# Attention followed by a gated MLP on one core: in the last batch, 32 by 32 block transposes on VectorE and a trip through DRAM in place of TensorE transposes

## Chip, cores and metric

The kernel runs on one core of a Trainium2 chip. The time is the device time of one execution in microseconds (us); a kernel's time is the median of its runs. The profile comes from one more execution, whose own time is named below.

## What is computed

```python
scores = scale * np.matmul(q, k.transpose(0, 1, 3, 2))      # (4, 12, 448, 64) each, fp32
scores = np.where(mask, -1000000000.0, scores)              # causal
attn = np.exp(scores - max) ; attn = attn / attn.sum
attn_out = np.matmul(attn, v)
x = attn_out.transpose(0, 2, 1, 3).reshape(1792, 768)
g = x @ w_gate ; val = x @ w_val                            # 768 -> 1536
out = (g * sigmoid(g) * val) @ w_out                        # 1536 -> 768
```

## The kernel before

The four batches are four chunks of 448 tokens. For each chunk, `attention(u)` runs once per head (a unit `u`; heads go in pairs, the even one with `h % 2 == 0`), and `moe(c)` is the MLP of the chunk. The attention of the last batch, b = 3, is spread between the MLP matmuls of the batch in front of it (b = 2).

Every piece of work is an `op` with the engines that it may run on, a cost, a due time and the buffers that it takes. A `Planner` goes through them and gives each engine its order; the instructions are then written in that order, and at run time each engine takes its own queue strictly in order. SP's queue issues the DMAs.

One head goes through these steps. `score` (L512): three fp32r matmuls per row block of a pair into PSUM tiles `S`. `rowmax` (L563, VectorE) adds the mask and takes the maximum of the row into `p`; `expo` (L575, ScalarE); `recip` (L587, L588, VectorE); `na`, `npl` or `nd` (L620, L624, L628) scales the rows of `p`. Then p, whose partitions are queries, must have keys on its partitions: `transp` (L710) makes three 128x128 TensorE transposes for key block 1 and three for blocks 2 and 3, and `transp0` (L678) four for the 64 keys of block 0, both heads of the pair at once, all into PSUM tiles `T`. `spread` copies each `T` to `ph` rounded to fp32r (L317 on ScalarE, L320 on VectorE) and puts the rest, `T` minus `ph`, into `pl` (L339). `weigh` multiplies by v: seven matmuls (L752) into the PSUM tile `O`, then a copy `tmp` and a sum into `xs`, from which `xh` and `xl` are split for the MLP.

The MLP's matmuls come in threes (L885 to L887), 448 columns each, 18 of them for one PSUM tile `M`. Their weights `whl` come by DMA from DRAM (L837, 768 KB each, five buffers); a load waits until TensorE is done with the buffer's last user.

Of the kernel before, what the change touches and what calls it, by code (L numbers as in the profile page):

```python
# [8 lines left out]
F32 = mybir.dt.float32  # L9
F32R = mybir.dt.float32r  # L10
U32 = mybir.dt.uint32
U16 = mybir.dt.uint16
# [4 lines left out]

P = 128
D = 64
BIG = -8.0e9  # L20
CUTS = [[0, 64, 192, 320, 448], [0, 64, 192, 320, 448], [0, 64, 192, 320, 448], [0, 64, 192, 320, 448]]
WID = [0, 64, 192, 320, 448]
# [25 lines left out]
TV = 0.0  # L48
WINDOW = 96
SPARE = [2]  # L50
FEW = 72
WARM = 22
WARM2 = 8
FIRST = [[[0, 1]], [[2]], [[3]]]
KBUS = 1 / 320
DLAT = 1.8
CAPS = {'S': 2, 'X': 2, 'T': 1, 'O': 1, 'M': 2, 'qraw': 3, 'kraw': 3, 'vraw': 3, 'QS': 1, 'KS': 1, 'VS': 3, 'ph': 2, 'pl': 2, 'p': 2, 'tmp': 2, 't': 3, 'osb': 2, 'wide': 3, 'wraw': 2, 'whl': 5}


def nat(flags, b, h):  # L60
# [17 lines left out]


class Op:  # L80
    __slots__ = ("port", "kind", "soft", "kb", "alts", "due", "deps", "alloc", "uses", "extra", "idx", "nd", "outs", "start", "end", "eng", "fn")

    def __init__(self, alts, due, deps, alloc, uses, extra):
        self.alts, self.due, self.alloc, self.uses, self.extra = alts, due, alloc, uses + alloc, extra
        self.deps = [d for d in deps if d is not None]
        self.port = False
        self.outs = []
        self.nd = len(self.deps)
        for d in self.deps:
            d.outs.append(self)  # L90
        for r in self.uses:
            r.left += 1


class Planner:
# [9 lines left out]
    def run(self, caps):  # L105
        free = dict.fromkeys(("PE", "DVE", "ACT", "POOL", "SP"), 0.0)
        ring = {}
        lock = {"DVE": 0.0, "POOL": 0.0}
        wire = 0.0
        kind = None  # L110

        def begin(o, e, t):
            if e == "POOL":
                return max(t, lock["DVE"])
            if e == "DVE" and o.port:
                return max(t, lock["POOL"])
            return t

        def slots(tag):
            if tag not in ring:  # L120
                c = caps.get(tag.rstrip("0123456789"), 1)
                ring[tag] = [None] * c
            return ring[tag]

        avail = {e: [] for e in free}

        def push(o):
            for e in o.alts:
                avail[e].append(o)
            dirty.update(o.alts)  # L130

        def ready(o, e):
            t = 0.0
            for d in o.deps:
                x = d.end if d in o.soft else d.end + d.extra + (LAT[d.eng] if d.eng != e else (0.0 if e == "PE" else 0.13))
                if x > t:
                    t = x
            for i, r in enumerate(o.alloc):
                h = slots(r.tag)[sum(x.tag == r.tag for x in o.alloc[:i])]
                if h is not None:  # L140
                    if h.left:
                        return None
                    if h.end > t:
                        t = h.end
            return t

        def extra(o, f):
            return BIAS.get(f, 0.0) + (SHARED if f == "DVE" and o.port else 0.0)

        def finish(o, e, s):  # L150
            best = s + o.alts[e][0] + extra(o, e)
            for f in o.alts:
                if f != e:
                    r = ready(o, f)
                    if r is not None and begin(o, f, max(r, free[f])) + o.alts[f][0] + extra(o, f) + 1e-6 < best:
                        return False
            return True

        def choose(e):
            lst = avail[e]  # L160
            lst.sort(key=lambda o: (o.due, o.idx))
            cand = []
            for o in lst[:WINDOW]:
                r = ready(o, e)
                if r is not None:
                    s = begin(o, e, max(r, free[e]))
                    if len(o.alts) == 1 or finish(o, e, s):
                        cand.append((s, o))
            if not cand:
                return None  # L170
            lim = max(min(s for s, _ in cand), free[e]) + DELTA[e]
            if e == "PE" and kind == "t":
                for s, o in cand:
                    if s <= lim and o.kind == "t":
                        return s, o
            for s, o in cand:
                if s <= lim:
                    return s, o
            return None

        dirty = set(free)
        for o in self.ops:
            if o.nd == 0:
                push(o)
        order = []
        left = len(self.ops)
        while left:
            best = None
            for e in free:
                c = choose(e)  # L190
                if c is not None and (best is None or (c[0], c[1].due) < (best[0], best[1].due)):
                    best = (c[0], c[1], e)
            assert best is not None
            s, o, e = best
            for f in o.alts:
                avail[f].remove(o)
            o.start, o.eng = s, e
            o.end = s + o.alts[e][0] * (GF if e == "POOL" else PF if e == "DVE" and o.port else 1.0)
            if e == "PE":
                o.end += TURN.get((kind or o.kind) + o.kind, 0.0)  # L200
                kind = o.kind
            o.fn = o.alts[e][1]
            free[e] = o.end
            if e == "SP":
                wire = max(wire, o.end) + o.kb * KBUS
                o.extra = wire + DLAT - o.end
            if e == "POOL" or (e == "DVE" and o.port):
                lock[e] = o.end
            for r in o.alloc:
                q = slots(r.tag)  # L210
                q.pop(0)
                q.append(r)
            for r in o.uses:
                r.left -= 1
                r.end = max(r.end, o.end + o.extra + LAT[e])
            for d in o.outs:
                d.nd -= 1
                if d.nd == 0:
                    push(d)
            order.append(o)  # L220
            left -= 1
        return order


def raw(t):
    return t.bitcast(F32)
# [3 lines left out]
def kernel(  # L230
# [115 lines left out]
    class Unit:  # L346
        def __init__(self, c, b, h, qa, qb, col):
            self.c, self.b, self.h, self.qa, self.qb, self.col = c, b, h, qa, qb, col
            cuts = CUTS[b]
            blocks = list(zip(cuts[:-1], cuts[1:]))  # L350
            self.kb = [e for e in blocks if e[0] < qb]
            self.qi = [(i, e) for i, e in enumerate(blocks) if qa <= e[0] < qb]
            self.rows = [e[1] - e[0] for _, e in self.qi]
            self.n = qb - qa
            self.ns, self.np = nat(NS, b, h), nat(NP, b, h)
            self.joint = self.ns and self.np
            self.own = [(i, e) for i, e in self.qi if i or h % 2 == 0 or not self.joint]

        def slot(self, j):
# [38 lines left out]
    def attention(u):  # L398
# [4 lines left out]
        nj = len(U.kb)  # L403
        frac = U.w0 / done_w[c]
        base = LEN[0] * FRAC0 * frac if c == 0 else start[c] + FRAC * LEN[c] * frac
        due = dues[u] = lambda stage: base + (SLOPE if c else SLOPE0) * stage
        if h % 2 == 0:
            def make(nm):
# [49 lines left out]
        if not npv:  # L458
            rV = Res("VS")

            def newv():
# [2 lines left out]
            v1 = op(copies("sbuf", nj * D, newv, lambda: s["v"]), due(8), [lv], [rV], [rv])  # L464
            v2 = op(binary(nj * D, lambda: s["VS"][:, :, D : 2 * D], lambda: s["v"],
                           lambda: raw(s["VS"])[:, :, 0:D]), due(9), [v1], [], [rV, rv])

        def peak(i):
            if "m" not in s:
# [58 lines left out]
        for i, (q0, q1_) in U.own:  # L528
# [17 lines left out]
            rp = ptile[u, i] if h % 2 else Res(f"p{sl}")  # L546
            so, rS = scored[u, i]
            new = h % 2 == 0
            if new and r < P:

                def newp(i=i, q1_=q1_, sl=sl):
                    s[f"pp{i}"] = st[u + 1][f"pp{i}"] = buf([P, 2 * q1_], F32, f"p{sl}", "p", f"p{u}_{i}")
# [81 lines left out]
        prps[u] = rps  # L634
        blocks = parts[u] = {}
        normed[u] = norms

        def spread(g, js, tr, rT, lo_row, kn, n, cols, offs, v2):

# [86 lines left out]
        if h % 2:  # L726
            weigh(u)

    def weigh(u):
        U = units[u]  # L730
        c, b, h, N = U.c, U.b, U.h, U.n
# [2 lines left out]
        k = h // 2  # L734
        prevx = [xlast[k]] if k in xlast else []
        if not npv:
            rO, dps, use, dur = Res("O"), [], [], 0.0
            for g, o_, w, _, stk, d_, r_ in (blocks[j] for j in range(nj)):
                dps += [x for x in d_ if x not in dps]
                use += [r for r in r_ if r not in use]  # L740
# [2 lines left out]
            todo = [(j, "ph") for j in (0, *range(2, nj))] + [(j, "pl") for j in range(nj - 1, 0, -1)] + [(1, "ph")]  # L743

            def pv():
                s["O"] = bank("O", f"O{u}")


                for x, (j, t) in enumerate(todo):
                    g, o_, w, _, stk, _, _ = blocks[j]  # L750
                    m = FEW if t == "pl" else 2 * D
                    nc.tensor.matmul(s["O"][:m, U.base(j) - U.qa : N], s["VS"][:, j, :m], s[f"{t}{g}"][:, o_ : o_ + w],  # L752
                                     start=x == 0, stop=x == len(todo) - 1)
            last = op({"PE": (dur, pv), "kind": "o"}, due(10), dps, [rO], use)
            rx, rt = Res(f"xs{h}"), Res("tmp")

# [280 lines left out]
```

## Time and profile before

| | |
|---|---|
| median of 3 runs | 674.75 us (674.54 to 675.5) |
| the profiled execution, its own time | 674.35 us |
| its span from first to last instruction | 672.5 us |
| TensorE busy | 666.1 us, 99% of the span |
| VectorE, ScalarE, GpSimd busy | 373.0, 357.4, 210.5 us |
| moved by DMA | 165.08 MB, 245 GB/s in the mean |

Matmuls are pipelined, so that the busy time of single ones overlaps; what a stretch of TensorE work costs is read from the distance between starts. The span is 1.85 us shorter than the execution's time.

### The profile page before, as it was taken

How to read it: one execution, taken by the hardware profiler on the slowest of the kernel's cores; microseconds unless marked ns; L12 is line 12 of the kernel's file. 1: busy time of each engine (PE TensorE's matmuls, PEld its weight loads, DVE VectorE, ACT ScalarE, POOL GpSimd, SP SyncE). 2: the span in 40 equal slices, each digit the busy share in tenths (PEclk: the TensorE clock that was granted, in tenths of full speed). 3: DMA queues.
4: the chain of work that ended last, by engine and by line, in shares of the span. 5: the costliest groups of instructions: out<-in, count | busy, mean ns of one | idle time of the engine just before them, and what ended most of it. 6: DMA issues, size and time to landing. Idle time of an engine off the chain costs nothing.

```text
span 672.5 us, 11031 instructions
## 1 busy us (share of the span) xinstructions
PE 666.1 (99%) x3906; PEld 601.9 (89%) x3906; DVE 373.0 (55%) x924; ACT 357.4 (53%) x877; POOL 210.5 (31%) x255
## 2 busy tenths in 40 slices
PE   9999999999999999999999999999999999999997
PEld 6568999999999999999999999999999999999997
DVE  5778978988886666766664355645534222222100
ACT  7998888789675674665653435545435211111000
POOL 3763445445333342462433314323422000000000
PEclk9999999999999999999999999999999999999999
DMA  8868886978958898968789766564466666656771
GB/s 292 302 197 283 305 272 241 310 263 309 353 186 304 287 318 275 313 213 300 266 298 342 268 205 211 160 208 158 148 211 207 214 207 228 210 215 232 221 244 42
DMA packets 45302, 165.08 MB, mean 245 GB/s; under 512 B 5056, under 2 KB 14528, under 8 KB 45248
## 3 DMA queue, kind: packets, MB, share of 16 engines
q1 hardware_dynamic: 45088, 164.29, 72.1%
q8 instruction: 31, 0.51, 0.3%
q14 instruction: 23, 0.19, 0.1%
q10 hardware_dynamic: 160, 0.10, 0.1%
HBM read 116.39 MB, written 47.97 MB: 244 GB/s over the span
## 4 chain that ended last, share of the span: by engine, by line
PE 95%; ACT 3%; DMA 0%; DVE 0%; issue 0%; POOL 0%; ACTq 0%; DVEq 0%
PE M L885 17%; PE M L886 17%; PE M L887 17%; PE MO L885 9%; PE MO L886 9%; PE MO L887 9%; PE S L512 6%; PE O L752 5%; PE T L710 4%; PE O L783 1%; PE T L678 1%; ACT p L575 1%; ACT p L620 1%; DMA kraw<-in_k_dram 0%; POOL p L624 0%
## 5 line engine op out<-in xcount | busy, mean ns | idle before, releaser
L885 PE MATMUL M<-xh,whl 128*128 128x448 f32 x576 | 215.3, 374 | 0.0
L886 PE MATMUL M<-xl,whl 128*128 128x448 f32 x576 | 209.3, 363 | 0.0
L887 PE MATMUL M<-xh,whl 128*128 128x448 f32 x576 | 209.1, 363 | 0.0
L887 PEld LDWEIGHTS M<-xh,whl 128*128 128x128 f32 x576 | 108.1, 188 | 7.7
L885 PEld LDWEIGHTS M<-xh,whl 128*128 128x128 f32 x576 | 108.2, 188 | 7.2 <-issue 0.3
L886 PEld LDWEIGHTS M<-xl,whl 128*128 128x128 f32 x576 | 108.4, 188 | 6.4
L885 PE MATMUL MO<-hh,whl 128*128 128x448 f32 x288 | 107.2, 372 | 0.0
L886 PE MATMUL MO<-hl,whl 128*128 128x448 f32 x288 | 104.6, 363 | 0.0
L887 PE MATMUL MO<-hh,whl 128*128 128x448 f32 x288 | 104.5, 363 | 0.0
L575 ACT ACTIVATE p<-p,m 128x192 f32<-128x192 f32 (+3 forms) x180 | 91.3, 512 | 3.0 <-DVE m L563 2.9
L563 DVE CUSTOM_DVE_ANT_0 p<-S,masks 128x192 f32<-128x192 f32 (+3 forms) x180 | 68.0, 426 | 16.2 <-PE S L512 15.8
L317 ACT ACTIVATE ph<-T 128x384 fp32r<-128x384 f32 (+3 forms) x93 | 46.6, 510 | 56.3 <-PE T L678 34.3
L317 ACT ACTIVATE hh<-t 128x448 fp32r<-128x448 f32 x43 | 24.8, 577 | 71.2 <-DVE t L928 71.2
L620 ACT ACTIVATE p<-p,rec 128x320 f32<-128x320 f32 (+3 forms) x136 | 59.9, 501 | 4.5 <-DVE rec L588 4.5
L339 DVE TENSOR_TENSOR whl<-wraw,whl 128x768 fp32r<-128x768 f32 x58 | 57.6, 993 | 7.1 <-ACT whl L317 5.9
L928 DVE TENSOR_TENSOR t<-t,M 128x448 f32<-128x448 f32 x48 | 29.7, 619 | 50.3 <-PE M L887 49.6
L922 DVE SCALAR_TENSOR_TENSOR t<-t,M 128x448 f32<-128x448 f32 x48 | 29.7, 619 | 50.2 <-ACT t L918 49.9
L887 PEld LDWEIGHTS MO<-hh,whl 128*128 128x128 f32 x288 | 54.0, 188 | 3.8
L885 PEld LDWEIGHTS MO<-hh,whl 128*128 128x128 f32 x288 | 54.1, 188 | 3.4
L886 PEld LDWEIGHTS MO<-hl,whl 128*128 128x128 f32 x288 | 54.2, 188 | 3.2
L918 ACT ACTIVATE t<-M 128x448 f32<-128x448 f32 x48 | 26.0, 542 | 47.0 <-PE M L887 46.2
L339 DVE TENSOR_TENSOR pl<-T,ph 128x384 fp32r<-128x384 f32 x72 | 39.6, 550 | 18.0 <-ACT ph L317 17.3
(81 smaller groups left out, 869.3 us busy)
## 6 DMA issues: line engine op xcount, KB each, us to landing
whl<-ws SPq DMA_DIRECT2D x72, 768.0 KB, 4.4
wide<-in_w_dram SPq DMA_DIRECT2D x36, 768.0 KB, 6.6
ws<-whl SPq DMA_DIRECT2D x36, 768.0 KB, 4.3
wr<-wraw SPq DMA_DIRECT2D x36, 384.0 KB, 3.5
wraw<-wr SPq DMA_DIRECT2D x36, 384.0 KB, 4.9
vraw<-in_v_dram SPq DMA_DIRECT2D x24, 256.0 KB, 3.6
out_dram<-osb SPq DMA_DIRECT2D x24, 224.0 KB, 4.5
qraw<-in_q_dram SPq DMA_DIRECT2D x23, 224.0 KB, 3.8
```

Source lines behind the costliest of these rows:

```text
L317: nc.scalar.activation(out(), in_(), AF.Copy, scale=scale)
L339: r["DVE"] = (cost("DVE", "two", n), lambda: nc.vector.tensor_tensor(out(), a(), b(), alu))
L512: nc.tensor.matmul(st[u + y][f"S{i}"][:r], Q[:, q0 : q0 + r], K[:, :q1_] if y else K[:, S - q1_ :], start=z == 0, stop=z == len(passes) - 1)
L563: nc.vector.tensor_tensor_reduce(p[:r], s[f"S{i}"][:r], mask[:r, maskX - q0 : maskX - q0 + q1_] if h % 2 else back[:r, P - min(q1_, P) : P ...
L575: nc.scalar.activation(p[:r], p[:r], AF.Exp, bias=peak(i)[:r], scale=-1.0, accum_out=sums[u % NR][:r, i : i + 1],)
L620: nc.scalar.activation(p[:r], p[:r], AF.Copy, scale=rec[u % NR][:r, i : i + 1])
L752: nc.tensor.matmul(s["O"][:m, U.base(j) - U.qa : N], s["VS"][:, j, :m], s[f"{t}{g}"][:, o_ : o_ + w], start=x == 0, stop=x == len(todo) - 1)
L885: nc.tensor.matmul(out[:, :n], a[:, w], xhi, start=first, stop=False)
L886: nc.tensor.matmul(out[:, :n], a[:, w], xlo, start=False, stop=False)
L887: nc.tensor.matmul(out[:, :n], l[:, w], xhi, start=False, stop=last)
L922: nc.vector.scalar_tensor_tensor(t, t, 1.0, ps[c, f, 0][:, :N], ALU.add, ALU.mult)
L928: nc.vector.tensor_tensor(t, t, ps[c, f, 1][:, :N], ALU.mult)
```

## The change

For the batches in `VIA`, here the last alone, `turn` replaces the TensorE transposes and `spread`. `blockwise` has VectorE transpose each 32x32 block of p in its place, 128 columns (four blocks) an instruction, from `p` into a buffer `w`: six instructions for the even head, ten for the odd one. `out` writes `w` to DRAM by 4 DMAs (even) or 10 (odd) so that the blocks come to lie under each other, `back` reads it all into SBUF by one DMA, and `pair` makes `ph` and `pl` from it. The queries of a row block come out in another order, which stays until the output; the host puts the columns of that batch back in order. The odd head's read also holds block 0 of both heads. `weigh` reads `ph` and `pl` by four pieces for key blocks 2 and 3. The due times of that batch's attention are 8 us earlier, and the odd head's `O` takes the PSUM bank that held `T`.

```diff
+VIA = [3]
+VLEAD = 8.0
+HOP = 0.8
...
                 wire = max(wire, o.end) + o.kb * KBUS
-                o.extra = wire + DLAT - o.end
+                o.extra = wire + DLAT + (HOP if o.hop else 0.0) - o.end
...
+        if U.via:
+            base -= VLEAD
...
+        if U.via:
+            turn(u, s, U, due, norms, rps)
...
+        n3 = 3 * G
...
+        nS = 3 * n3 + G if odd else 2 * n3
+        tps = []
+        for i in range(0 if odd else 1, 4):
+            def blockwise(i=i):
...
+                r = U.rows[i]
+                for t in range(i, 2 * i + 1) if odd else range(i):
...
+                    nc.vector.transpose(s["stage"][:r, :, at : at + G],
+                                        s[f"pp{i}"][:r, P * t : P * t + P].rearrange("p (c n) -> p c n", c=4))
...
+        row = 4 * n3 + 2 * G if odd else 0
+        ND = row + 8 * n3 if odd else 8 * n3
+
+        def out():
+            d = s["d"] = dpool.tile([P, ND], F32, tag=rD.tag, name=f"{rD.tag}{u}", bufs=CAPS[rD.tag])
+            to = d.rearrange("(c i) n -> i c n", c=4)
+            for b in range(4):
+                f = s["stage"][G * b : G * b + G]
+                if odd:
+                    nc.sync.dma_start(to[:, :, n3 * b : n3 * b + n3], f[:, :, :n3])
+                    if b < 2:
+                        nc.sync.dma_start(to[:, :, 4 * n3 + G * b : 4 * n3 + G * b + G], f[:, :, 3 * n3 :])
+                nc.sync.dma_start(to[:, :, row + 2 * n3 * b : row + 2 * n3 * (b + 1)], f[:, :, n3 * odd : n3 * odd + 2 * n3])
...
+            t = s["w"][:, 0 if odd else 4 * nS :][:, :ND]
+            s["turned"] = t
+            nc.sync.dma_start(t, s["d"])
...
+            hi = op(copies("sbuf", n, newh, view), due(8), [tr], [rh], [res])
...
+            lo = op(binary(n, newl, view, lambda: part(raw(s[f"ph{g}"])[r0 : r0 + kn])), due(9), [hi],
...
-            rO, dps, use, dur = Res("O"), [], [], 0.0
+            rO, dps, use, dur = Res("T" if U.via and h % 2 else "O"), [], [], 0.0
...
+                    if U.via:
+                        o, p = s["O"][:m, :N], s[f"{t}{g}"]
+                        if j:
+                            o, p = (x_[:, : 12 * G].rearrange("p (b n) -> p b n", b=4) for x_ in (o, p))
+                            o = o[:, :, G * (j - 1) :]
+                            p = p[:, :, : 3 * G - G * (j - 1)] if j < 3 else p[:, :, 2 * G :]
```

In the orders below a row is an instruction, its output, its inputs and its size; a name ends in a number that the program gave. On TensorE before, this is the end of an even head of the last batch, its product with v (`O`), and one group of the odd head's transposes behind it, between MLP matmuls (`M`).

```order
L887 MATMUL M_16_5466<-xh_82,whl_5270 128x448
L752 MATMUL O_5503<-ph_0_5486,VS_5078 128x448
L752 MATMUL O_5503<-ph_2_5425,VS_5078 128x256
L752 MATMUL O_5503<-ph_2_5425,VS_5078 128x128
L752 MATMUL O_5503<-pl_2_5430,VS_5078 72x128
L752 MATMUL O_5503<-pl_2_5430,VS_5078 72x256
L752 MATMUL O_5503<-pl_1_5406,VS_5078 72x384
L752 MATMUL O_5503<-ph_1_5399,VS_5078 128x384
L710 MATMUL T_1_5515<-ident,p_1_5324 128x128
L710 MATMUL T_1_5515<-ident,p_2_5326 128x128
L710 MATMUL T_1_5515<-ident,p_3_5333 128x128
L885 MATMUL M_17_5524<-xh_77,whl_5370 128x448
```

In the change the same head's product stands there with the odd head's product right behind it (L868 is the matmul of `weigh`, L1000 to L1002 the MLP's).

```order
L1002 MATMUL M_17_5612<-xh_80,whl_5400 128x448
L868 MATMUL O_5649<-ph_0_5591,VS_5140 128x448
L868 MATMUL O_5649<-ph_2_5507,VS_5140 128x4x64
L868 MATMUL O_5649<-ph_2_5507,VS_5140 128x4x32
L868 MATMUL O_5649<-pl_2_5542,VS_5140 72x4x32
L868 MATMUL O_5649<-pl_2_5542,VS_5140 72x4x64
L868 MATMUL O_5649<-pl_1_5512,VS_5140 72x384
L868 MATMUL O_5649<-ph_1_5505,VS_5140 128x384
L868 MATMUL O_5659<-ph_0_5581,VS_5442 128x448
```

The 96 transposes of the last batch are gone from TensorE; 4 of the 7 products of a head now take four pieces, with as many columns as before.

On SP's queue before, at the start of the last batch's attention, there are only weight loads, an output store and the inputs of the next pair.

```order
L960 DMA out_dram<-osb_5_4711 128x448
L837 DMA whl_4778<-ws_160 128x1536
L422 DMA qraw_4795<-in_q_dram 128x448
L422 DMA kraw_4809<-in_k_dram 128x448
L837 DMA whl_4824<-ws_161 128x1536
L837 DMA whl_4872<-ws_162 128x1536
L837 DMA whl_4895<-ws_163 128x1536
```

In the change, at the same place, the first pair's writes (`dE` even, `dO` odd) and reads stand between them (L952 is the weight load, L796 the read).

```order
L786 DMA dE_4799<-w_4783 32x4x192 x4
L952 DMA whl_4824<-ws_160 128x1536
L783 DMA dO_4843<-w_4814 32x4x96
L785 DMA dO_4843<-w_4814 32x4x32
L786 DMA dO_4843<-w_4814 32x4x192
...
L783 DMA dO_4843<-w_4814 32x4x96
L786 DMA dO_4843<-w_4814 32x4x192
L796 DMA w_4783<-dE_4799 128x768
L952 DMA whl_4880<-ws_161 128x1536
L952 DMA whl_4888<-ws_162 128x1536
L952 DMA whl_4911<-ws_163 128x1536
L796 DMA x_4941<-dO_4843 128x1216
```

Three weight loads now stand behind the odd head's ten writes and the even head's read, and the odd head's read stands behind those three.

## Rows read from the trace of the kernel before

**Rows 1.** The page: span, busy time by engine, TensorE in 40 slices.

```profile
span 672.5 us, 11031 instructions
...
PE 666.1 (99%) x3906; PEld 601.9 (89%) x3906; DVE 373.0 (55%) x924; ACT 357.4 (53%) x877; POOL 210.5 (31%) x255
...
PE   9999999999999999999999999999999999999997
```

**Rows 2.** Three stretches: length, busy time by engine, granted clock, DMA share, GB/s.

```profile
345.60:369.00 23.40, 23.40 (x142) 21.77 (x143) 12.67 (x36) 12.16 (x33) 9.84 (x11) 1.00 0.91 318
...
430.00:456.00 26.00, 26.00 (x159) 24.01 (x158) 13.10 (x37) 13.01 (x34) 7.97 (x12) 1.00 0.54 182
...
540.00:672.50 132.50, 128.86 (x645) 120.63 (x643) 22.40 (x36) 16.78 (x30) 0.00 (x0) 1.00 0.62 203
```

**Rows 3.** TensorE's timeline around one transpose group: start, duration, instruction.

```profile
437.70 0.36 PE L886 MATMUL M<-xl,whl 128*128 128x448 f32 x1
437.90 0.36 PE L887 MATMUL M<-xh,whl 128*128 128x448 f32 x1
438.10 0.49 PE L710 MATMUL T<-ident,p 128*128 128x128 f32 x3
438.35 0.45 PE L885 MATMUL M<-xh,whl 128*128 128x448 f32 x1
438.63 0.37 PE L886 MATMUL M<-xl,whl 128*128 128x448 f32 x1
```

**Rows 4.** The critical chain, 425 to 457 us: start, time on the chain.

```profile
430.03 1.72 PE S L512 x22
...
438.26 0.33 PE T L710 x3
...
448.54 0.44 PE T L678 x4
448.98 0.21 PE M L885
...
451.45 0.93 PE O L752 x7
```

**Rows 5.** VectorE's groups by form, 369 to 540 us.

```profile
L563 DVE CUSTOM_DVE_ANT_0 p<-S,masks 128x192 f32<-128x192 f32 x12 | 4.1, 345 | 0.0
...
L563 DVE CUSTOM_DVE_ANT_0 p<-S,masks 64x64 f32<-64x64 f32 x12 | 2.6, 214 | 12.5 <-PE S L512 12.5
```

**Rows 6.** Timelines of VectorE and ScalarE behind the scores of one pair.

```profile
405.16 0.22 DVE L563 CUSTOM_DVE_ANT_0 p<-S,masks 64x64 f32<-64x64 f32 x1 [1.18 <-PE S L512]
...
409.33 1.01 ACT L620 ACTIVATE p<-p,rec 128x192 f32<-128x192 f32 x2
...
412.93 1.36 ACT L620 ACTIVATE p<-p,rec 64x64 f32<-64x64 f32 x3 [0.95 <-DVE rec L588]
...
422.99 1.09 ACT L317 ACTIVATE ph<-T 64x448 fp32r<-64x448 f32 x2 [1.60 <-PE T L678]
```

**Rows 7.** The page on DMA: packets, the main queue, issues with time to landing.

```profile
DMA packets 45302, 165.08 MB, mean 245 GB/s; under 512 B 5056, under 2 KB 14528, under 8 KB 45248
...
q1 hardware_dynamic: 45088, 164.29, 72.1%
...
whl<-ws SPq DMA_DIRECT2D x72, 768.0 KB, 4.4
...
wr<-wraw SPq DMA_DIRECT2D x36, 384.0 KB, 3.5
wraw<-wr SPq DMA_DIRECT2D x36, 384.0 KB, 4.9
```

**Rows 8.** SP's queue: one issue, and its waits from 365 to 545 us.

```profile
427.70 0.33 SPq L422 DMA_DIRECT2D vraw<-in_v_dram  x1
...
SPq L837 <- PE M L887: 87.2, 24, 7.6
```

**Rows 9.** Tile T: TensorE transposes into contiguous (L710) and split (L676) columns.

```profile
L710 PE MATMUL T<-ident,p x288: 270/272/331, 10.3 to 534.5; 128*128 128x128 f32 x144
...
L676 PE MATMUL T<-ident,p x6: 271/300/329, 11.4 to 49.0; 128*128 128x128 f32 x6
```

More of the change, by code (lines that the diff above doesn't have):

```diff
@@ L19 @@
 D = 64
+G = 32
 BIG = -8.0e9
@@ L56 @@
 DLAT = 1.8
-CAPS = {'S': 2, 'X': 2, 'T': 1, 'O': 1, 'M': 2, 'qraw': 3, 'kraw': 3, 'vraw': 3, 'QS': 1, 'KS': 1, 'VS': 3, 'ph': 2, 'pl': 2, 'p': 2, 'tmp': 2, 't': 3, 'osb': 2, 'wide': 3, 'wraw': 2, 'whl': 5}
+CAPS = {'S': 2, 'X': 2, 'T': 1, 'O': 1, 'M': 2, 'qraw': 3, 'kraw': 3, 'vraw': 3, 'QS': 1, 'KS': 1, 'VS': 3, 'ph': 2, 'pl': 2, 'p': 2, 'tmp': 2, 't': 3, 'osb': 2, 'wide': 3, 'wraw': 2, 'whl': 5, 'dE': 2, 'dO': 2}
 def nat(flags, b, h):
@@ L80 @@
 class Op:
-    __slots__ = ("port", "kind", "soft", "kb", "alts", "due", "deps", "alloc", "uses", "extra", "idx", "nd", "outs", "start", "end", "eng", "fn")
+    __slots__ = ("hop", "port", "kind", "soft", "kb", "alts", "due", "deps", "alloc", "uses", "extra", "idx", "nd", "outs", "start", "end", "eng", "fn")
     def __init__(self, alts, due, deps, alloc, uses, extra):
@@ L85, in __init__ @@
         self.deps = [d for d in deps if d is not None]
-        self.port = False
+        self.port = self.hop = False
         self.outs = []
@@ L356, in __init__ @@
             self.joint = self.ns and self.np
+            self.via = b in VIA
             self.own = [(i, e) for i, e in self.qi if i or h % 2 == 0 or not self.joint]
@@ L466, in attention @@
                            lambda: raw(s["VS"])[:, :, 0:D]), due(9), [v1], [], [rV, rv])
+            s["v2"] = (v2, rV)
         def peak(i):
@@ L548, in attention @@
             new = h % 2 == 0
-            if new and r < P:
+            if new and r < P and not U.via:
                 def newp(i=i, q1_=q1_, sl=sl):
@@ L636, in attention @@
         normed[u] = norms
+        if U.via:
+            turn(u, s, U, due, norms, rps)
+            if h % 2:
+                st[u - 1]["later"]()
+                weigh(u - 1)
+                weigh(u)
+            return
         def spread(g, js, tr, rT, lo_row, kn, n, cols, offs, v2):
@@ L727, in attention, with turn, back, pair @@
             weigh(u)
+    def turn(u, s, U, due, norms, rps):
+        h, blocks = U.h, parts[u]
+        odd = h % 2
+        n3 = 3 * G
+        rS = Res("wide")
+        wide = lambda nm: buf([P, 4 * WC + 4], U16, "wide", "wide", nm).bitcast(F32)
+        nS = 3 * n3 + G if odd else 2 * n3
+        tps = []
+        for i in range(0 if odd else 1, 4):
+            def blockwise(i=i):
+                if "stage" not in s:
+                    s["w"] = wide(f"w{u}")
+                    s["stage"] = s["w"][:, : 4 * nS].rearrange("p (c n) -> p c n", c=4)
+                r = U.rows[i]
+                for t in range(i, 2 * i + 1) if odd else range(i):
+                    j = t - i if odd else i - t
+                    at = n3 * odd + n3 * (j >= 2) + G * (2 if j == 3 else i - j) if j else (3 * n3 if i == 0 else G * (i - 1))
+                    nc.vector.transpose(s["stage"][:r, :, at : at + G],
+                                        s[f"pp{i}"][:r, P * t : P * t + P].rearrange("p (c n) -> p c n", c=4))
+            k = i + 1 if odd else i
+            deps = [norms[i]] + ([normed[u - 1][i]] if odd else [])
+            new = not tps
+            o = op({"DVE": (k * (0.06 + P / 960), blockwise)}, due(6.2), deps + tps[:1], [rS] * new, [rps[i]] + [rS] * (not new))
+            o.soft = o.soft + tps[:1]
+            tps.append(o)
+        rD = Res("dO" if odd else "dE")
+        row = 4 * n3 + 2 * G if odd else 0
[10 more added lines that the diff above has]
+                nc.sync.dma_start(to[:, :, row + 2 * n3 * b : row + 2 * n3 * (b + 1)], f[:, :, n3 * odd : n3 * odd + 2 * n3])
+        wr = op({"SP": (3.4 if odd else 1.4, out), "kb": 800 if odd else 450}, due(6.4), tps, [rD], [rS])
+        wr.hop = True
+        rP = Res("wide") if odd else rS
+        def back():
+            if odd:
+                s["w"] = wide(f"x{u}")
+            t = s["w"][:, 0 if odd else 4 * nS :][:, :ND]
+            s["turned"] = t
+            nc.sync.dma_start(t, s["d"])
+        rd = op({"SP": (0.35, back), "kb": ND // 2}, due(6.6), [wr], [rP] if odd else [], [rD] + ([] if odd else [rS]))
+        rd.hop = True
+        v2, rV = s["v2"]
+        N = U.n
+        def pair(g, view, res, r0, kn, n, tr):
+            stk = kn == D
+            rh = Res(f"ph{g}")
+            part = (lambda t: t) if stk else (lambda t: t.rearrange("p (b n) -> p b n", b=4))
+            def newh():
+                s[f"ph{g}"] = buf([P, n], F32R, f"ph{g}", "ph", f"ph{u}_{g}")
+                return part(s[f"ph{g}"][r0 : r0 + kn])
+            hi = op(copies("sbuf", n, newh, view), due(8), [tr], [rh], [res])
+            rl = None if stk else Res(f"pl{g}")
+            def newl():
+                if stk:
+                    return s[f"ph{g}"][D - r0 : P - r0]
+                s[f"pl{g}"] = buf([P, n], F32R, f"pl{g}", "pl", f"pl{u}_{g}")
+                return part(s[f"pl{g}"])
+            lo = op(binary(n, newl, view, lambda: part(raw(s[f"ph{g}"])[r0 : r0 + kn])), due(9), [hi],
+                    [] if stk else [rl], [res, rh])
+            for j in ([0], [1], [2, 3])[g]:
+                blocks[j] = (g, 0, N if stk else 4 * G * (4 - j), slice(0, P), stk, [hi, lo, v2], [rh, rV] + ([] if stk else [rl]))
+        groups = lambda k: lambda: s["turned"][:, row : row + 8 * n3].rearrange("p (b n) -> p b n", b=4)[:, :, n3 * k : n3 * k + n3]
+        if odd:
+            joint = lambda r0: lambda: s["turned"][r0 : r0 + D, :N]
+            pair(0, joint(D), rP, D, D, N, rd)
+            def later():
+                e = st[u - 1]
+                e["first"](joint(0), rP, rd)
+            st[u - 1]["later"] = later
+        else:
+            s["first"] = lambda view, res, tr: pair(0, view, res, 0, D, N, tr)
+        for g in (1, 2):
+            pair(g, groups(g - 1), rP, 0, P, 4 * n3, rd)
@@ L745, in pv @@
             def pv():
-                s["O"] = bank("O", f"O{u}")
+                s["O"] = bank(rO.tag, f"O{u}")
                 for x, (j, t) in enumerate(todo):
@@ L751, in pv @@
                     m = FEW if t == "pl" else 2 * D
-                    nc.tensor.matmul(s["O"][:m, U.base(j) - U.qa : N], s["VS"][:, j, :m], s[f"{t}{g}"][:, o_ : o_ + w],
-                                     start=x == 0, stop=x == len(todo) - 1)
+                    o, p = s["O"][:m, U.base(j) - U.qa : N], s[f"{t}{g}"][:, o_ : o_ + w]
+                    if U.via:
[4 more added lines that the diff above has]
+                            p = p[:, :, : 3 * G - G * (j - 1)] if j < 3 else p[:, :, 2 * G :]
+                    nc.tensor.matmul(o, s["VS"][:, j, :m], p, start=x == 0, stop=x == len(todo) - 1)
             last = op({"PE": (dur, pv), "kind": "o"}, due(10), dps, [rO], use)
@@ L1035 @@
     r = _run(nc, [arrays], core_ids=[0])
-    return _np.ascontiguousarray(r.results[0]["out_0_dram"].T)
+    out = r.results[0]["out_0_dram"].T.copy()
+    for b in VIA:
+        x = _np.arange(S)
+        q = _np.where(x < S - D, CUTS[b][1] + x % 96 // G * P + x // 96 * G + x % G, x - (S - D))
+        out[b * S + q] = out[b * S + x]
+    return _np.ascontiguousarray(out)
```

## The prediction

> **What bounds the kernel.** The page first: TensorE is busy for 99% of the span, all but the first and last slices at nine tenths, while VectorE and ScalarE have nearly half of theirs free [rows 1]. Busy time of pipelined matmuls can hide gaps, so I read stretches next. In 430 to 456 us, one pair of the last batch, TensorE has no idle time at the full clock, VectorE and ScalarE are busy for 13 of 26 us, DMA for 0.54 [rows 2]. So in the stretch that the change touches TensorE's own queue is the limit and every microsecond taken from it shortens the run, if nothing that it then waits for is late.
>
> **What is removed.** Two MLP matmuls in a row start 0.20 us apart. Across a group of three transposes the starts are 438.10 (the group), 438.35 and 438.63 [rows 3]: from the group's start to the second matmul it is 0.53 us where 0.20 is normal, so the group costs 0.33 us, and the critical chain gives the same 0.33; the group of four costs 0.44 [rows 4]. A pair has four groups of three and one of four: 4 x 0.33 + 0.44 = 1.76 us. Six pairs: **10.56 us**. Behind the group of four the chain also shows twelve MLP matmuls in 451.45 - 448.98 = 2.47 us instead of 2.40 [rows 4]; if that goes as well it is 0.07 x 6 = 0.4 us more. I take nothing for it.
>
> **What TensorE gets instead.** The product with v keeps its columns, but 4 of its 7 matmuls read and write four pieces. The nearest row is the transpose into split columns, 300 ns against 272 [rows 9]: at most 0.028 x 4 x 12 heads = 1.3 us. I take 0, since the split row comes from six instructions in another part of the kernel whose extremes (271 to 329) are those of the unsplit row; 1.3 is the other end.
>
> **VectorE.** 16 block transposes a pair, 128 columns each. No row shows one. The mask-and-maximum instruction takes 214 ns for 64 columns and 345 for 192 [rows 5]; halfway is 280 ns, and with such instructions starting some 0.07 us before the last one ends I count 0.25 us apart: 1.5 us for the even head, 2.5 for the odd one, 4 us a pair on an engine with 13 us free [rows 2]. The copies out of PSUM that go make up for part. Nothing of it lies on TensorE's path by itself; it counts in the chain below.
>
> **DMA and SP.** Per pair 14 writes and 2 reads: 16 issues of 0.33 us [rows 8], 5.3 us of SP's queue in 26. Even: 512 runs of 768 bytes (393 KB); odd: 512 runs of 384, 256 of 128 and 512 of 768 bytes (1280 runs, 623 KB). Written and read that is 2.03 MB in 26 us, 78 GB/s on top of 182; the sum of 260 is below the 318 that an earlier stretch moved with no gap on TensorE [rows 2]. Bandwidth is not the question; the time of short runs is. Nothing before has such DMAs. From below by bytes: 318 GB/s at a share of 0.91 is 350 in all, 21.8 a DMA engine, so an odd run of 486 bytes in the mean takes 22 ns. From above: a packet of this kernel takes 0.721 x 16 x 672.5 / 45088 = 0.172 us [rows 1, 7], and it carries 3.6 KB. I take **0.05 us a run**, nearer to the bytes because the packets here are seven times as long: 80 odd runs on each of 16 engines are then 4.0 us, between 1.8 and 13.8.
>
> **Does the product with v find its operands?** This decides. All that follows counts from the end of a pair's scores, by the pair whose scores end just ahead of 405.16 [rows 6]. Even rows are scaled by 410.34, +5.2; odd ones by 414.29, +9.2. Even: transposes to +6.7, four issues to +8.0. Odd: transposes to +11.7, ten issues to +15.0. In the first pair SP has the even read behind these: issued at +15.3, landed 4.9 us later (the 384 KB reload [rows 7]) at +20.2. The odd writes land at +18.5 (3.5 us after the last issue, the 384 KB store [rows 7]; 4 us of runs from +11.7 on, with the same latency, end about there too). The odd read goes out at +18.8 and lands at +23.7; if the weight loads ahead of it have bunched up, two more of 2.25 us each (768 KB at 350 GB/s) make it +28.2. Then two copies to `ph` (1.09 us [rows 6]), one subtraction and the handing over between engines, about 2 us: the even head's operands stand at **+25.7 to +30.2**.
>
> TensorE comes to that product, by the order of the change, after 147, 168, 138, 150, 141 and 147 MLP matmuls in the six pairs, beside other scores (1.72 us) and products (0.93 [rows 4]): 31.1, 37.2, 31.2, 33.6, 31.8 and 31.2 us. The cover is 0.9 to 5.4 us longer than the chain in the tightest pairs. The odd head's product comes at once or three matmuls later and needs two more copies and subtractions, split over engines, so its slack is about half a microsecond less. I therefore expect little waiting: 1 us in all.
>
> **What is queued behind the new waits.** SP holds weight loads while it waits for the transposes. Before, SP waits for TensorE to free a buffer (24 waits, 87.2 us in the stretch [rows 8]), so loads go out as early as they can. Five buffers of 18 matmuls at 0.20 us are 18 us; less the buffer in use (3.6) and the load itself (4.4 [rows 7]) a load can be 10 us late. SP is held from about +8 to +15.3, some 7 us: covered at no cost, and each microsecond above 10 would be one on TensorE. On ScalarE the copies that wait for a read stand ahead of exponentials of the next pair and of the MLP's tanh, which frees an `M` bank; they come late only when the product does, and the two waits then overlap.
>
> **Sum.** Profiled execution 674.35 - 10.56 + 1.0 = 664.8 us. Its span of 672.5 becomes 662.9 with the same 1.85 us around it. The median of the runs is 0.4 us above the profiled execution: **665.2 us**. No waiting and the 0.4 of rows 4 give 663.8; the split columns at their upper end and 0.5 us of waiting a pair give 668.5.
>
> **A rule against the change.** The critical chain prices a transpose on TensorE at 0.11 us (0.33 for three) on the engine that is full [rows 1, 4]. The Trainium skill, "VectorE: DVE Perf Modes", section "Rules for kernel authors", says to do a 128x128 transpose on TensorE if PSUM will do as its destination, and to use VectorE for 32x32 blocks. By the row the removed work is worth 10.56 us; by the rule the trip that joins the blocks should cost more than that and the time would end above 674.75. The rule counts the transpose itself, not which engine is full, so I go by the row.
>
> **Rivals.**
> (a) *Late trip, part given back.* What speaks for it: all six pairs depend on the trip, the tightest slack is under 1 us, and ten issues in a row may wait for earlier ones' semaphores. At 0.09 us a run the odd write ends 80 x 0.04 = 3.2 us later; less a slack of about 2 us it is 1.2 us a pair, 7 on top of 664.2 without waiting: 671.4.
> (b) *Short runs cost like packets, slower than before.* The place is the odd write, the wait is in front of the even head's product. The gain is 1.76 us a pair; with 2 us of slack it is gone when the write is 3.8 us late, at 0.05 + 3.8/80 = 0.097 us a run. At 0.13 it is 6.4 - 2 - 1.76 = 2.6 us a pair worse, 16 in all: 690; at the upper bound of 0.172 it is 9.8 - 3.76 = 6 us a pair: 711. Against it: the run lengths are a seventh of the packets'.
> (c) *Short runs are done twice.* The trace's packets under 512 bytes are too few and too mixed to price [rows 7]. If a run under 512 bytes needs two passes, 48 of the 80 odd runs on an engine cost another 0.05 us: 2.4 us later, 0.4 us a pair beyond the slack of 2, 2.4 in all, or 9 with the slack at 0.9: 667 to 674. The Trainium skill, "DMA: Bandwidth & Descriptors", section "Specifications", says that below 512 B an SDMA engine reads, modifies and writes.
> (d) *SP holds the weights too long.* If SP is held 12 us instead of 7, each pair loses 2 us: 676. Against it: 10 us of cover per load.
>
> **Chances.** Forecast as summed, 663 to 668.5: 0.60, with the mild end of (c) in it. Part given back, 668.5 to 673.4 ((a), the far end of (c)): 0.18. Within 0.2% of before, 673.4 to 676.1 ((a) at its break-even): 0.08. Slower ((b), (d)): 0.14. About 0.2% is what a measurement of this kernel can tell from no change. Faster is then 0.78, same 0.08, slower 0.14. The range from 663.0 to 674.0 leaves out 0.18: (b), (d) and most of the even case.
>
> **What would show it.** Right: no TensorE transposes in the last 300 us; MLP matmuls 0.20 us apart through the last batch; no idle time on TensorE in front of its products; the MLP of the last chunk starting about 10 us sooner and taking as long; odd reads landing at most 28 us behind their scores. Wrong: idle time of TensorE released by the subtractions into `ph` or by a DMA into `x`, equal in each pair (a, b, c), or by `whl` (d); odd writes that land over 8 us after their first issue; products of a head above 0.93 us (split columns); block transposes far from 0.25 us.

## The result

The changed kernel takes **664.73 us** (median of 4 runs, 663.92 to 666.8); the kernel before, run beside it, 675.05 us. The ratio is 0.9852, with an interval of 0.9827 to 0.9877: 10 us faster. 665.2 us was forecast.

The page of the changed kernel, its first lines and its main DMA queue (share of 16 engines), answers to [rows 1] and [rows 7]:

```profile
span 662.5 us, 11097 instructions
...
PE 655.9 (99%) x3810; PEld 592.9 (90%) x3810; DVE 383.1 (58%) x999; ACT 359.3 (54%) x885; POOL 214.5 (32%) x262
...
PE   9999999999999999999999999999999999999997
...
q1 hardware_dynamic: 58912, 176.48, 78.1%
```

96 matmuls are gone from TensorE, which is as full as before; VectorE has 10 us more work, which costs nothing. The span is 10.0 us shorter. The timelines place it: the last chunk's MLP starts at 529.0 us instead of 539.1, and takes 133.4 us in both.

Three stretches of the changed kernel (columns as in [rows 2]), the middle one with the third pair of the last batch:

```profile
400.00:430.00 30.00, 30.00 (x171) 27.95 (x170) 18.94 (x67) 17.34 (x46) 12.10 (x19) 1.00 0.88 296
430.00:456.00 26.00, 25.87 (x153) 23.84 (x152) 16.57 (x51) 14.45 (x39) 10.73 (x15) 1.00 0.82 268
...
530.00:662.50 132.50, 128.78 (x644) 120.50 (x643) 22.93 (x37) 16.78 (x30) 0.00 (x0) 0.99 0.61 203
```

TensorE has no idle time but 0.13 us in the middle stretch; DMA is at 0.82 to 0.88 in the first two instead of 0.60 and 0.54. The critical chain shows that one place. It leaves TensorE and goes through the trip of the third pair (start, time on the chain; L783 and L796 are the odd head's writes and the reads, L327 and L346 GpSimd's copy and subtraction):

```profile
431.38 5.69 DMA dO<-w
437.09 0.30 SPq L783
...
439.52 8.24 DMA x<-dO
447.91 0.57 POOL ph L327
448.56 0.57 POOL ph L327
449.20 1.16 POOL ph L346
450.43 1.17 POOL ph L346
451.64 2.12 PE O L868 x14
```

The last matmul ahead of this product starts at 451.15, so that 451.35 would have been its time: it waited 0.29 us for GpSimd, which takes 1.16 us for a subtraction where VectorE takes 0.65 (the mean of nine of the same form). In the other five pairs nothing waits.

### The profile page after: what moved, and what is told of

Same layout as the page of the kernel before. It is cut to its first block, busy times and chain, and to the rows that moved or that the text cites. A ratio compares the mean times of both kernels' runs of the same rounds, so it can differ in the third digit from the quotient of the medians.

```text
span 662.5 us, 11097 instructions
## 1 busy us (share of the span) xinstructions
PE 655.9 (99%) x3810; PEld 592.9 (90%) x3810; DVE 383.1 (58%) x999; ACT 359.3 (54%) x885; POOL 214.5 (32%) x262
## 4 chain that ended last, share of the span: by engine, by line
PE 91%; ACT 3%; DMA 3%; POOL 1%; DVE 1%; issue 1%; SPq 0%; ACTq 0%; DVEq 0%; POOLq 0%
PE M L1000 16%; PE M L1001 16%; PE M L1002 16%; PE MO L1000 9%; PE MO L1001 9%; PE MO L1002 9%; PE S L520 6%; PE O L868 5%; PE T L726 3%; PE O L898 1%; ACT p L583 1%; DMA x<-dO 1%; ACT p L628 1%; PE T L694 1%; DMA dO<-w 1%
## 5 line engine op out<-in xcount | busy, mean ns | idle before, releaser
L1000 PE MATMUL M<-xh,whl 128*128 128x448 f32 x576 | 213.9, 371 | 0.0
L1002 PE MATMUL M<-xh,whl 128*128 128x448 f32 x576 | 209.0, 363 | 0.0
L1002 PEld LDWEIGHTS M<-xh,whl 128*128 128x128 f32 x576 | 108.1, 188 | 7.6
L1000 PEld LDWEIGHTS M<-xh,whl 128*128 128x128 f32 x576 | 108.2, 188 | 7.5 <-issue 0.3
L1000 PE MATMUL MO<-hh,whl 128*128 128x448 f32 x288 | 106.6, 370 | 0.0
L1002 PE MATMUL MO<-hh,whl 128*128 128x448 f32 x288 | 104.5, 363 | 0.0
L571 DVE CUSTOM_DVE_ANT_0 p<-S,masks 128x192 f32<-128x192 f32 (+3 forms) x180 | 67.6, 425 | 15.4 <-PE S L520 15.1
L1037 DVE SCALAR_TENSOR_TENSOR t<-t,M 128x448 f32<-128x448 f32 x48 | 29.7, 618 | 48.8 <-ACT t L1033 48.4
L1002 PEld LDWEIGHTS MO<-hh,whl 128*128 128x128 f32 x288 | 54.0, 188 | 3.8
L1000 PEld LDWEIGHTS MO<-hh,whl 128*128 128x128 f32 x288 | 54.1, 188 | 3.4
L321 ACT ACTIVATE ph<-T 128x384 fp32r<-128x384 f32 (+3 forms) x74 | 36.8, 510 | 27.9 <-PE T L694 17.3
L632 POOL TENSOR_SCALAR p<-p,rec 128x448 f32<-128x448 f32 (+3 forms) x45 | 29.0, 650 | 53.6 <-DVE rec L596 26.5
```

Source lines behind the costliest of these rows:

```text
L321: nc.scalar.activation(out(), in_(), AF.Copy, scale=scale)
L571: nc.vector.tensor_tensor_reduce(p[:r], s[f"S{i}"][:r], mask[:r, maskX - q0 : maskX - q0 + q1_] if h % 2 else back[:r, P - min(q1_, P) : P ...
L1000: nc.tensor.matmul(out[:, :n], a[:, w], xhi, start=first, stop=False)
L1002: nc.tensor.matmul(out[:, :n], l[:, w], xhi, start=False, stop=last)
L1037: nc.vector.scalar_tensor_tensor(t, t, 1.0, ps[c, f, 0][:, :N], ALU.add, ALU.mult)
```

## The experiments

Profiles also differ ahead of the last batch, where the change and most of these edits leave TensorE's work alone: the last product of the third batch starts between 368.7 and 370.4 us. So some results below also give the time from that start to the end of the span, as "behind the third batch". It is 303.2 us before and 292.5 in the changed kernel: 10.7 us less.

**Only the due times.** The kernel before with the attention of the last batch due 8 us earlier.

```diff
+        if b == 3:
+            base -= 8.0
         due = dues[u] = lambda stage: base + (SLOPE if c else SLOPE0) * stage
```

> The kernel before, with the due times of the last batch's attention 8 us earlier and nothing else of the change. Theory (the gain is TensorE time of the removed transposes): no gain, 674 to 676 us. Rival (the gain comes from the other order, in which scores run earlier and products wait less): 665 to 671 us.

674.98 us, ratio 1.0 (0.9991 to 1.0009), and 303.4 us behind the third batch. The earlier due times by themselves gain nothing.

**The transposes put back.**

```diff
                 s["O"] = bank(rO.tag, f"O{u}")
+                for x in range(8 * U.via):
+                    nc.tensor.transpose(s["O"][:, P * (x % 3) : P * (x % 3) + P], ident, ident)
```

> The changed kernel with eight fp32 transposes of the identity, unused, put on TensorE ahead of each product of the last batch: 96 in all, as many as were removed, with nothing that waits for them. Theory: the 10.6 us come back, at 0.11 us each: 674.5 to 676 us. Rival (TensorE had room, the gain came from the order, from the second PSUM bank for the product or from the copies out of PSUM): under 670 us.

674.28 us, ratio 0.9991 (0.9982 to 1.0001), level with before. The trip, VectorE's transposes, the new order and the second bank are all still in it: it is the 96 transposes on TensorE that make the 10 us. The median is 0.2 us under the expected range and 9.6 above the changed kernel's; behind the third batch the profiles are 303.0 and 292.5 us long, 10.5 apart. One group of eight and the MLP matmul behind the product that follows it:

```profile
405.28 1.04 PE L857 MATMUL O<-ident 128*128 128x128 f32 x8
...
407.06 0.37 PE L1002 MATMUL M<-xh,whl 128*128 128x448 f32 x1
```

That is 1.78 us from start to start, of which the product is 0.91: 0.87 for eight, 0.11 each, as in the groups of three [rows 4].

**No trip.** Without the writes and reads the blocks are not joined.

```diff
...
+                if r < P:
+                    nc.vector.memset(s["stage"][r:, :, 3 * n3 :], 0.0)
...
         def out():
+            return
...
-            if odd:
-                s["w"] = wide(f"x{u}")
-            t = s["w"][:, 0 if odd else 4 * nS :][:, :ND]
-            s["turned"] = t
-            nc.sync.dma_start(t, s["d"])
+            s["turned"] = s["w"][:, :ND]
```

> The changed kernel without its 84 writes and 12 reads through DRAM: the copies read the blocks where VectorE left them, so the blocks are not joined and the products use wrongly placed data; one small memset a pair is added. Theory (trip hidden but for 0.3 us in the third pair): 664 to 665 us, no gain. Rival (the trip slows others, by DMA load, SP's queue or contention): 660 to 663 us.

663.16 us (663.11 to 663.48), ratio 0.9827 (0.9812 to 0.9841). That is 1.6 us below the changed kernel by the medians, between the ranges of theory and rival; the intervals of the two ratios overlap, the times of the single runs do not. From the last product of the third batch on, where the trip begins to matter, the profile is 292.1 us long, 0.4 under the changed kernel's. The changed kernel with 12 us of lead (below) keeps its trip and has 292.1 us too, so the trip as such costs TensorE nothing there. The other 0.7 us between the two profiles lie ahead of that point; whether the edit has a part in them is not shown. From 369 to 530 us the share of DMA is 0.63 without the trip and 0.86 with it.

**A later trip.** Six, and in another run three, writes to an unused place ahead of the odd head's ten; all orders kept.

```diff
+            if odd:
+                e = dpool.tile([P, 2 * n3 * 6], F32, tag="dX", name=f"dX{u}", bufs=2)
+                for x in range(6):
+                    nc.sync.dma_start(e.rearrange("(c i) n -> i c n", c=4)[:, :, 2 * n3 * x : 2 * n3 * (x + 1)], s["stage"][:G, :, n3 : 3 * n3])
```

> The changed kernel with six more writes of 96 KB to an unused place ahead of each odd head's ten, the order of all engines kept: the odd trip starts some 2.6 us later (0.43 us an issue). Theory (slack about 1 us in each pair, none in the third, as the trace after shows): 1.6 us a pair of waiting, 10 in all, 672 to 677 us, idle time of TensorE in front of its products. Rival (slack of 3 us or more): at most 667 us.

> As the run with six extra writes, with three: the odd trip starts some 1.3 us later, order of all engines kept. Theory (slack of about 1 us in each pair, none in the third): 0.3 us of waiting in most pairs and 1.6 in the third, 2 to 4 us in all, 666 to 669 us; above that only if the MLP's matmuls fall into their slower spacing of 0.2067 us. Rival (each late microsecond costs one in all pairs): 672 us.

With six 677.73 us (672.7 to 680.6), ratio 1.0028 (0.9998 to 1.0058): the whole gain is gone. With three 671.77 us (667.6 to 677.3), ratio 0.9958 (0.993 to 0.9985): 7 us lost, where the theory had 2 to 4. The number is the rival's, 672, so only the waits can decide. TensorE's waits for the products' operands, first with six, then with three (who waited for whom, us, times, longest):

```profile
PE O L872 <- DVE ph L343: 4.1, 2, 2.3
PE O L872 <- POOL ph L346: 3.6, 2, 3.3
```

```profile
PE O L872 <- POOL ph L346: 3.0, 1, 3.0
PE O L872 <- DVE ph L343: 2.3, 2, 2.2
```

With three, two pairs wait long (3.0 and 2.2 us), one 0.2 us and three not at all. That is not the rival's equal wait in every pair; the small slack holds, but the theory's 0.3 us in most pairs and 1.6 in the third is wrong too. The waits are 5.4 us with three and 7.7 with six; behind the third batch the profiles are 301.2 and 306.8 us long, 8.7 and 14.3 above the changed kernel's. So more is lost than the waits. One part is the clock. Four stretches of the profile with six, the first three around its longest wait:

```profile
448.00:452.00 4.00, 4.00 (x22) 3.75 (x21) 2.83 (x15) 1.57 (x6) 1.15 (x2) 1.00 0.99 372
452.00:456.00 4.00, 0.69 (x5) 0.31 (x3) 2.07 (x8) 3.82 (x11) 3.38 (x4) 1.00 0.91 378
456.00:460.00 4.00, 4.00 (x17) 3.86 (x18) 3.04 (x8) 2.94 (x10) 1.42 (x3) 0.57 0.48 118
...
536.00:540.00 4.00, 4.00 (x26) 3.78 (x25) 2.45 (x5) 1.37 (x3) 0.29 (x1) 1.00 0.59 244
```

TensorE is busy for 0.69 of 4 us, and in the next 4 us the granted clock is 0.57 in the mean: most of that time at 1.2 instead of 2.4 GHz. With three writes the same stands behind both long waits:

```profile
456.00:459.00 3.00, 3.00 (x14) 2.83 (x13) 2.13 (x6) 2.16 (x6) 1.42 (x3) 0.60 0.22 56
...
533.00:537.00 4.00, 4.00 (x18) 3.78 (x17) 1.62 (x3) 1.08 (x2) 0.00 (x0) 0.57 0.40 167
```

It does not stand behind every wait: with six the clock is 1.00 behind the last one, of 2.3 us (536 to 540 us above). The other part is the pace of the MLP, told at the end; of these two profiles it came in the one with six alone. With three writes the last pair shows why 1.3 us of issues became more: its odd read goes out 7.1 us later on the clock than in the changed kernel, of which 4.3 us are the run's own lag; the writes of the longer row wait for one another, and the read leaves 2.8 us late.

**Two batches.**

```diff
-VIA = [3]
+VIA = [2, 3]
```

> The changed kernel with the last two batches by VectorE and DRAM. TensorE loses another 10.6 us of transposes. Theory (the change pays only where DMA has room; in the third batch's stretch DMA already moved about 300 GB/s, and 78 more pass what it moves at a full share, about 350): the trip and the weights are late there, over 664.7 us, 668 to 690. Rival (only TensorE's work counts): 654 to 656 us.

691.66 us, ratio 1.0241 (1.021 to 1.0272), 1.7 us past the expected range. The third batch's stretch before, and in two parts in this run:

```profile
215.00:345.60 130.60, 130.60 (x771) 120.19 (x767) 88.53 (x211) 81.85 (x200) 53.27 (x62) 1.00 0.83 283
```

```profile
215.00:345.00 130.00, 118.44 (x701) 103.70 (x701) 103.19 (x324) 93.85 (x243) 53.38 (x69) 0.99 0.90 310
345.00:369.00 24.00, 19.66 (x101) 17.00 (x100) 18.95 (x57) 17.80 (x45) 8.39 (x12) 0.86 0.96 349
```

Who waited for whom in the same run:

```profile
PE M L1000 <- ACT whl L321: 5.2, 3, 3.6
PE M L1002 <- DVE whl L343: 4.9, 7, 1.4
PE M L1000 <- DMA whl<-ws: 2.6, 1, 2.6
```

DMA reaches 349 GB/s at a share of 0.96. Of TensorE's 26 us of waits some 19 are for the MLP's weights, which share the queue with the trip, and few for the products. The first two rows are the splitting of weights on ScalarE and VectorE: from 215 to 345 us the unsplit weights land 6.3 us after the issue in the median, against 5.0 in the same stretch before. Behind the waits the clock falls as well (0.86 in the second part).

**Two batches with half the weight traffic.** The MLP's weights are not kept split in DRAM (768 KB each); every chunk after the first loads them unsplit (384 KB) and splits them.

```diff
-VIA = [3]
+VIA = [2, 3]
...
-RAW = [1]
+RAW = []
```

> As the run with two batches, and the MLP's split weights are no longer stored to DRAM in the second chunk and loaded whole by the later ones: each chunk loads the unsplit weights, half the bytes, and splits them again. Theory (DMA room is what decides): DMA has room in both stretches, faster than with the split weights stored; 655 to 662 us if the splitting finds room on VectorE, ScalarE and GpSimd, which are then the next limit. Rival: no better than the run with two batches alone.

660.31 us, ratio 0.9782 (0.9767 to 0.9796): 31 us from the run before it by this edit alone. The third batch's stretch:

```profile
215.00:345.00 130.00, 125.28 (x742) 113.93 (x741) 103.28 (x316) 98.50 (x247) 59.45 (x67) 1.00 0.69 205
```

VectorE and ScalarE are at least as busy as in the run before, so it was not their load that held the weights up; the unsplit weights now land in 3.8 us. The edit also takes stores out of SP's queue; what these issues cost by themselves is not shown.

**That edit without the change.** `RAW = []` in the kernel before.

> The kernel before, all transposes on TensorE, with the MLP's split weights not stored: each chunk loads the unsplit ones and splits them. It parts the two edits of the run with two batches. Theory (that edit only makes room for DMA; TensorE's work is the same): within 1 us of before, 674 to 676. Rival (it is itself the gain of that run): 660 to 666 us.

674.45 us, ratio 1.0 (0.999 to 1.001). Less DMA is worth nothing to the kernel with TensorE transposes, and decides whether the trip pays with two batches.

**More lead.** `VLEAD = 12.0` in the changed kernel, and in the one with two batches and unsplit weights.

> The changed kernel with the last batch's attention due 12 us earlier than before instead of 8, for more cover of the trip. Theory (only about 0.4 us of the trip is uncovered): 663.5 to 665 us, no idle time ahead of a product. Rival (the trip costs more by late products than the profile shows): under 663 us.

> The run with two batches and unsplit weights, with attention of both batches due 12 us earlier instead of 8. Theory (the 4.7 us that TensorE idles in the third batch's stretch are products and weights that come late): more cover takes part of it back, 656 to 660 us. Rival (the splitting of the weights is what is late there): no change, 660 to 661, or slower.

For one batch 664.42 us (663.54 to 664.71), ratio 0.9842 (0.9828 to 0.9857): level with 8 us of lead, as expected, with no wait ahead of a product in the last batch. For two batches **654.35 us** (653.51 to 655.07), ratio 0.970 (0.9686 to 0.9715): the fastest, 10 us below the changed kernel and better than the 656 to 660 expected. Its third batch's stretch:

```profile
215.00:345.00 130.00, 128.91 (x764) 117.89 (x763) 102.11 (x306) 95.75 (x239) 55.90 (x59) 1.00 0.67 202
```

TensorE idles 1.1 us of 130, against 4.7 with 8 us of lead. Of those 4.7 us the expectation named the products (1.7) and the weights (1.0) and missed the longest wait, 2.1 us of scores for VectorE's row maximum. VectorE is at 79% in both.

## Why the prediction held, step by step

**TensorE is the limit, 10.56 us come off it.** Right, though of the 40 slices only the last is under nine tenths, not the first: the transposes put back cost 10.5 us behind the third batch, the earlier due times alone gain nothing. The 0.4 us that I left out (slower MLP matmuls behind the group of four) is in the gain too: these stretches are gone, and 10.56 + 0.4 less 0.3 of waiting is the 10.7 us measured there. The forecast took 9.56 us off the span; that the span shows 10.0 has a share of chance, since in this execution the third batch ended 0.6 us later than before.

**The products in four pieces.** Right at 0. A product takes 0.91 us on the chain where nothing waits, no more than the 0.93 before [rows 4]:

```profile
478.51 0.91 PE O L868 x7
480.03 0.91 PE O L868 x7
```

**VectorE.** 280 ns forecast; by form:

```profile
L765 DVE STREAM_TRANSPOSE w<-p 128x128 f32<-128x128 f32 x90 | 19.9, 276 | 3.5 <-ACT p L628 2.3 <-POOL p L632 0.6
```

Six in a row take 1.27 us in the timeline, 0.20 us each from start to start (0.25 forecast).

**The trip.** Right up to the issue of the reads in the first pair, with two terms off in opposite ways; too short behind it. In the first pair, whose scores end at 375.16, SP's queue shows (start, duration):

```profile
384.62 0.30 SPq L783 DMA_DIRECT2D dO<-w  x1
...
389.85 0.43 SPq L786 DMA_DIRECT2D dO<-w  x1
390.56 0.34 SPq L796 DMA_DIRECT2D w<-dE  x1
...
393.32 0.32 SPq L796 DMA_DIRECT2D x<-dO  x1
```

The first odd write goes out at +9.5 (11.7 forecast: the odd head's first block transposes start at 381.40, +6.2, while its later rows are still being scaled), the even read at +15.4 (15.3), the odd read at +18.2 (18.8). The ten issues take longer than forecast, 0.43 us each with a wait between: each DMA waits until the one eight places before it is done. Here the eighth odd write goes out at 388.75, and the weight load eight places ahead of it landed at 388.73. SP's waits of this kind from 360 to 535 us:

```profile
SPq L786 <- DMA whl<-ws: 3.0, 3, 1.4
```

In the other five pairs the odd read goes out later, at +19.4 to +23.6. The landing is longer as well. Issues from 360 to 535 us (count, KB, median us to landing):

```profile
whl<-ws SPq DMA_DIRECT2D x42, 768.0 KB, 5.7
x<-dO SPq DMA_DIRECT2D x6, 608.0 KB, 7.5
...
dO<-w SPq DMA_DIRECT2D x24, 96.0 KB, 2.7
...
dO<-w SPq DMA_DIRECT2D x24, 48.0 KB, 3.3
...
dO<-w SPq DMA_DIRECT2D x12, 16.0 KB, 3.9
```

The odd read takes 7.5 us instead of 4.9, in a queue at 0.86; that is the bunch of weight loads that I had as the far end. It lands at +26.3 in the first pair and up to +29.7 in the others, in three of the six past the 28 that I had named as a sign of being right. The copies and subtractions behind it take longer too: in the first pair they begin at 403.58, 2.1 us after the landing, since other work stands ahead of them in ScalarE's order, and the subtraction ends at 405.48, 4.0 us after the landing where I had 2. So the even head's operands stand at +30.3 in the first pair, the far end of my 25.7 to 30.2, and past it in four of the others. TensorE reaches the first product at 406.6, +31.4 (31.1 forecast), 1.1 us after the even head's last subtraction. In five pairs the slack, worked out in this way, is 0.9 to 1.6 us; the third is 0.29 late. I had 0.9 to 5.4 and 1 us of waiting in all; it was 0.3. That so long a chain cost so little is partly luck: the runs with extra writes show what another microsecond or two would have done.

**Short runs.** From the queue's row against [rows 7]: 0.781 x 16 x 662.5 - 0.721 x 16 x 672.5 = 521 us of engine time for 13,824 packets more and 12.19 MB more: **38 ns a packet** of 882 bytes in the mean, 40 by the bytes at 21.8 GB/s an engine. Reads and 1,536 packets of 4 bytes are in this mean. The trace also has the size and time of each single packet. In the mean the 128-byte runs of the changed kernel's queue took 13 ns, those of 384 bytes 25 and those of 768 bytes 43 (36 in the median). An odd run, 486 bytes in the mean, is thus 30 ns where I took 50, and the 80 on an engine take 2.4 us instead of 4.0. Rival (b), up to 172, was wrong. Of (c), another 50 ns for a short run, nothing is seen: a 384-byte run is dearer than its bytes (18 ns at 21.8 GB/s an engine), but not by a second pass of that length. The Trainium skill, "DMA: Bandwidth & Descriptors", section "Specifications", has runs under 512 B read, modified and written; if that happens here, it is not in the packets' own time.

**Rivals (a) and (d).** (a) named the right danger: the runs with extra writes show that a trip some 2.8 us longer costs 7 us, and a little more the whole gain. My price, one microsecond of waiting per microsecond late, was too low: with three extra writes 5.4 us of waits came with 8.7 us of loss. (d) did not come: no weight load kept TensorE waiting in the changed kernel.

**The rule against the change.** The Trainium skill, "VectorE: DVE Perf Modes", section "Rules for kernel authors", gives 128x128 transposes to TensorE. Here it does not hold: TensorE was the only full engine, and 96 transposes less on it are worth 10 us. With two batches and the split weights in the same queue it would have been right, at 691.66 us.

## What to carry over

When one engine is full without a gap, price what leaves it by the distance between starts in its own queue (0.11 us a transpose here, not the 0.27 us of the instruction), then ask only whether what it waits for next can be late. A detour through DRAM cost 0.4 us here, and nothing with 4 us more lead, while there was room in DMA; check room and lead in the very stretch, since the same edit loses 17 us where DMA is nearly full and wins 20 with other traffic cut and more lead. A late product can cost more than its wait: behind some of the waits TensorE came back at a lower clock.

## What I had not expected of the hardware

The MLP's matmuls, 448 columns at the full granted clock, have two paces. The last chunk in the changed kernel, and in the run with six extra writes (timeline, first and last of 30 and of 61 matmuls):

```profile
529.01 0.36 PE L1000 MATMUL M<-xh,whl 128*128 128x448 f32 x1
...
534.82 0.36 PE L1002 MATMUL M<-xh,whl 128*128 128x448 f32 x1
```

```profile
539.47 0.37 PE L1004 MATMUL M<-xh,whl 128*128 128x448 f32 x1
...
551.87 0.37 PE L1004 MATMUL M<-xh,whl 128*128 128x448 f32 x1
```

That is 0.2003 and 0.2067 us from start to start. In the second run the slower pace came with the product that followed a wait of 2.35 us and stayed to the end: 648 matmuls x 0.0067 = 4.3 us, beside 7.7 us of waits. It is about the pace that [rows 4] show behind the groups of four, where it ends at the next product. A wait is not needed for it: in the run with the due times alone it holds for 38 matmuls from 460.4 us on, and in the run with the transposes put back for 44 from 409.5 on, where TensorE waits for nothing. The clock is 1.00 at both paces. What sets it I could not tell. It is not all of the spread of the late runs either: with three extra writes the profile has the faster pace through the last chunk, and the runs still spread from 667.6 to 677.3 us.
